# Taking the low part of a weight tile in two GpSimd operations of 512 columns instead of one of 1024

## The chip, the core and the metric

The kernel runs on one core of one Trainium2 chip. Time is device time in microseconds (us) of a whole launch, with all transfers. Five engines work side by side, each through its own list of instructions in a fixed order, and wait for each other by semaphores: TensorE (PE: matmuls, PEld: its weight loads), VectorE (DVE), ScalarE (ACT), GpSimd (POOL) and SyncE (SP, which only issues transfers here). An instruction whose inputs aren't ready holds up everything that stands behind it on its engine.

## What is computed

Three layers follow each other. The first is attention over 4 batches, 8 heads, 576 positions and 64 features per head, in which each query keeps only its 32 largest scores. The other two are MLPs over the 2304 tokens, 512 to 2048 to 512 features, each with its own gate. Cut to what matters:

```python
scores = scale * q @ k.T                       # per batch and head, 576 x 576
kth = partition(scores, -32)[..., -32]         # the 32nd largest of each row
attn = softmax(where(scores >= kth, scores, -1e9))
x = (attn @ v) as 2304 x 512
h = x @ w_in;  x = (h - tanh(h)) @ w_out                        # first MLP
h = x @ w_in;  x = where(h > 0, h, exp(min(h, 0)) - 1) @ w_out  # second MLP
```

## The kernel before

**Tokens in chunks.** The 2304 tokens go through in 6 chunks of 384. For each chunk, 4 pairs of heads are computed: scores `ps` (TensorE), copied to `s` (ScalarE), then four rounds of finding the 8 largest (`vm`, VectorE MAX8, line 406) and striking them out (`w`, VectorE, line 420), exponentials `e` (line 410 or 423 on ScalarE, masked on VectorE at line 427, or masked on ScalarE), transposes `pt` copied to `ph`, and the product `av` with the values. The result, normalised, is the chunk's `x`, kept as a high part `xh` and a low part `xl`. While one chunk's MLPs run on TensorE, the attention of later chunks runs on VectorE and ScalarE, so that the two share every engine.

**Numbers in two parts.** Matmuls take a number as high part plus low part. ScalarE copies the number into the rounded format (high), and GpSimd subtracts that from the number (low). The helper `split` does both, at lines 148 and 149, and so all of these operations have the same two lines in the profile: `gh` and `gl` (gated values), `kh`/`kl` in the tile `kk` (keys), `xl`, and the weights `wp`.

**The MLPs.** An MLP (`m` = 0 or 1) goes through 16 f-tiles (`ft`) of 128 hidden features. A step of it is: 12 matmuls of 384 columns at line 577 (`first`) into `h`, which has 2 buffers; a tanh or exponential `t` on ScalarE; a gate `g` on VectorE (line 596 in the first MLP, 591 in the second), which reads `h` and so releases its buffer; `gh` and `gl`; and 9 matmuls of 512 columns at line 613 (`second`) into `acc`. So `h` of step k+2 can't start before the gate of step k is done.

**The weights.** A f-tile's weights are a tile of 128 x 2 x 2 x 512: two halves of 512 columns (the first for `h`, the second for `acc`), each with a high and a low part. Chunk 0 makes them (`prepare`): a transfer brings the raw words `wr`; two operations on ScalarE (lines 186 and 203) and one on VectorE (line 189) make the number `wf` of 1024 columns out of them; ScalarE rounds it (`wp`, line 148), GpSimd takes the low part (`wp`, line 149), and a transfer at line 213 stores the whole tile. There are 32 of these, 16 for each MLP. All other chunks load the stored tiles (`wt`, line 222, 1 MB each) into a ring of 6 buffers. The first 12 tiles are made with the VectorE operation in two halves that read ScalarE's result from PSUM (`sc`); the 20 others with one of 1024 columns, both of whose inputs lie in SBUF.

**What sets the order.** The program is written in ticks, four for each group of query tiles, with tables that say in which tick each piece is written. Then a scheduler places the instructions on each engine by its own estimates of how long they take, so that an instruction which it thinks is longer or shorter moves its neighbours, and these theirs.

Of the kernel before, what the change touches and what calls it, by code (L numbers as in the profile page):

```python
# [106 lines left out]
def tile_topk_attention_two_mlps(  # L107
# [9 lines left out]
    nc = tc.nc  # L117
# [24 lines left out]
    copy = AF.Copy  # L142

    def f(ap):
        return ap.bitcast(F32)

    def split(hi, lo, src):
        nc.scalar.activation(hi, src, copy)  # L148
        return nc.gpsimd.tensor_sub(lo, src, f(hi))  # L149
# [7 lines left out]
    def bank(tag, name, bufs):  # L157
        if tag == "h":
            if "park" in pairs:
                turns.close()  # L160
                del pairs["park"]
                pairs["h"] = pool("ph", 1, PSUM)
            return pairs["h"].tile([P, 512], F32, tag=tag, name=name, bufs=bufs)
        return ps.tile([P, 512], F32, tag=tag, name=name, bufs=bufs)
# [7 lines left out]
    def weight_tile(name):  # L172
        return sb.tile([P, 2, 2, 512], F32R, tag="w", name=name, bufs=W2_BUFS)
# [3 lines left out]
    def prepare(m, ft):  # L177

        raw = sb.tile([P, 1024], I64, tag="wr", name=f"wr{m}_{ft}", bufs=RAW_BUFS)
        nc.sync.dma_start(raw, (w1, w2)[m][ft])  # L180
        words = raw.bitcast(F32).rearrange("p (n w) -> p n w", w=2)
        low, scaled = words.bitcast(U32)[:, :, 0], words[:, :, 1]
        w = sb.tile([P, 1024], F32, tag="wf", name=f"wf{m}_{ft}", bufs=WF_BUFS)

        def scale(out, src):
            nc.scalar.activation(out, src, AF.Prelu, scale=2.0**-112, alpha=-(2.0**32))  # L186

        def join(out, high, low):
            nc.vector.scalar_tensor_tensor(  # L189
                out.bitcast(U32), high.bitcast(U32), 3, low, op0=ALU.logical_shift_left, op1=ALU.bitwise_or  # L190
            )

        halves = [slice(0, 512), slice(512, 1024)]
        small = {}
        early = "wide" in stage
        if early:
            for a, cs in enumerate(halves):
                small[a] = bank(f"acc{stage['at'] % 3}", f"sc{m}_{ft}_{a}", 1)
                stage["at"] += 1
                scale(small[a], scaled[:, cs])  # L200
        else:
            scale(scaled, scaled)
        nc.scalar.activation(low.bitcast(I32), low, copy, scale=2.0**-29 * (1 - 2.0**-20), bias=-0.5 + 7.5 * 2.0**-20)
        if early:
            for a, cs in enumerate(halves):
                join(w[:, cs], small[a], low[:, cs])
        else:
            join(w, scaled, low)
        wt = weight_tile(f"wp{m}_{ft}")
        if m * NF + ft not in EARLY:  # L210
            weights[0, m, ft] = wt
        split(wt[:, :, 0], wt[:, :, 1], w.rearrange("p (h c) -> p h c", h=2))
        nc.sync.dma_start(f(scratch[m, ft]), f(wt))

    def load_next():
        if loads:
            ci, m, ft = loads.pop(0)
            if ci == 0 and m * NF + ft not in EARLY:
                prepare(m, ft)
                return  # L220
            wt = weights[ci, m, ft] = weight_tile(f"wt{ci}_{m}_{ft}")
            newest["weights"] = nc.sync.dma_start(f(wt), f(scratch[m, ft]))
# [508 lines left out]
    for tick in range(FIRST_TICK, n_ticks):  # L731
        for do in before.get(tick, ()):
            do()
        while early and PREP_AT + PREP_RATE * (len(EARLY) - len(early)) <= tick:
            i = early.pop(0)
            prepare(i // NF, i % NF)
# [16 lines left out]
        for j in range(max(1, len(todo))):  # L753
            a, b, c = todo[j] if todo else (lambda: None,) * 3
# [58 lines left out]
```

## Time and profile before

| | |
|---|---|
| runs | 1219.96, 1218.08, 1215.3 us |
| median of them | 1218.08 us |
| the profiled execution | 1219.57 us |
| its span, first to last instruction | 1217.8 us |
| TensorE busy | 1146.4 us, 94% of the span |
| VectorE busy | 944.5 us, 78% |
| ScalarE busy | 765.6 us, 63% |
| GpSimd busy | 497.9 us, 41% |
| mean granted TensorE clock | 0.973 |

The shares are means over unlike stretches. Up to about 150 us there is only attention and the making of weights, and TensorE is far from full. From 150 to about 215 us the first MLP of chunk 0 starts beside attention, VectorE is full, and TensorE has its last larger waits. From there on TensorE is busy 98% and more, and from about 1025 us there is little but MLPs.

### The profile page before, as it was taken

What the parts mean: (1) busy time and instruction counts of PE and PEld (TensorE: products, weight loads), DVE (VectorE), ACT (ScalarE), POOL (GpSimd) and SP (SyncE); (2) the same over time, 40 slices, a digit from 0 to 9 for tenths busy, and PEclk for the clock granted to TensorE, in tenths of its full rate; (3) what the DMA queues carried; (4) which work ended last, traced back from release to release, by engine and by line L of the source; (5) the groups of instructions that cost most, each with busy time, mean ns of one, the idle gap of its engine ahead of it and who ended that gap; (6) DMA issues with size and microseconds to landing.
All of it is one profiled execution on the core that took longest, in us unless ns stands there. A gap on an engine that the chain in (4) does not pass through costs nothing.

```text
span 1217.8 us, 18856 instructions
## 1 busy us (share of the span) xinstructions
PE 1146.4 (94%) x6349; PEld 977.0 (80%) x6349; DVE 944.5 (78%) x1898; ACT 765.6 (63%) x1594; POOL 497.9 (41%) x557
## 2 busy tenths in 40 slices
PE   6577689999999999999999999999999999999998
PEld 3344368888888979898978988988998888898887
DVE  7999999998999999679987789898889995100111
ACT  5999987888984555565664566575655564432333
POOL 2445446657753313443423444444334422333222
PEclk9688889999999999999999999999999999999999
DMA  7999937985979986669986779978688645686572
GB/s 246 398 333 330 311 111 276 350 266 217 356 285 327 276 294 184 238 166 299 241 182 234 242 204 260 251 219 266 225 241 243 204 127 207 210 283 248 198 269 95
DMA packets 81616, 301.69 MB, mean 248 GB/s; under 512 B 18800, under 2 KB 36080, under 8 KB 51696
## 3 DMA queue, kind: packets, MB, share of 16 engines
q1 hardware_dynamic: 81520, 300.49, 76.5%
q8 instruction: 50, 0.82, 0.3%
q14 instruction: 46, 0.38, 0.1%
HBM read 255.07 MB, written 45.39 MB: 247 GB/s over the span
## 4 chain that ended last, share of the span: by engine, by line
PE 75%; ACT 6%; DVE 5%; DMA 3%; issue 1%; POOL 1%; another core or an unknown queue 0%; ACTq 0%; DVEq 0%; POOLq 0%
PE h L577 30%; PE acc L613 30%; PE av L470 6%; PE pt L448 5%; DMA wt<-w 3%; PE ps L383 2%; PE ps L384 2%; DVE vm L406 2%; DVE w L420 2%; DVE wf L189 1%; ACT ph L449 1%; ACT s L385 1%; ACT e L410 1%; ACT y L627 1%; ACT wr L186 0%
## 5 line engine op out<-in xcount | busy, mean ns | idle before, releaser
L149 POOL TENSOR_TENSOR gl<-g,gh 128x384 fp32r<-128x384 f32 x192 | 205.3, 1071 | 385.0 <-ACT gh L148 360.2
L406 DVE MAX8 vm<-w 128x8 f32<-128x576 f32 x432 | 315.0, 748 | 3.1
L613 PE MATMUL acc<-wt,gh 128*128 128x512 f32 x1014 | 270.9, 398 | 0.3 <-ACT gh L148 0.3
L613 PEld LDWEIGHTS acc<-wt,gh 128*128 128x128 f32 x1014 | 186.2, 188 | 34.9 <-issue 3.3
L420 DVE MATCH_REPLACE8 w<-vm,w 128x576 f32<-128x576 f32 x288 | 212.7, 740 | 0.0
L148 ACT ACTIVATE gh<-g 128x384 fp32r<-128x384 f32 x192 | 100.7, 525 | 81.2 <-DVE g L591 34.6
L613 PE MATMUL acc<-wt,gl 128*128 128x512 f32 x507 | 148.9, 398 | 1.0 <-POOL gl L149 1.0
L577 PE MATMUL h<-zh,wt 128*128 128x384 f32 (+2 forms) x776 | 146.4, 324 | 2.4 <-ACT zh L632 2.0
L591 DVE SCALAR_TENSOR_TENSOR g<-t,h 128x384 f32<-128x384 f32 x96 | 52.2, 544 | 124.2 <-ACT t L583 123.8
L406 DVE MAX8 vm<-s 128x8 f32<-128x576 f32 x144 | 107.2, 750 | 47.1 <-ACT s L385 44.4
L577 PE MATMUL h<-xh,wt 128*128 128x384 f32 x672 | 140.9, 339 | 1.2 <-DMA wt<-w 1.2
L385 ACT ACTIVATE s<-ps 128x288 f32<-128x288 f32 (+1 forms) x272 | 107.5, 418 | 48.3 <-PE ps L384 40.7
L449 ACT ACTIVATE ph<-pt 116x384 f32<-116x384 f32 (+1 forms) x240 | 111.5, 499 | 40.0 <-PE pt L448 37.4
L448 PE MATMUL pt<-ident,e 128*116 128x128 f32 (+1 forms) x720 | 115.2, 288 | 22.7 <-ACT e L423 9.9
L577 PEld LDWEIGHTS h<-zh,wt 128*128 128x128 f32 x776 | 125.8, 189 | 8.8 <-ACT zh L632 3.2
L448 PEld LDWEIGHTS pt<-ident,e 128*116 128x116 f32 (+1 forms) x720 | 90.0, 142 | 43.2 <-ACT e L423 12.6
L577 PEld LDWEIGHTS h<-xh,wt 128*128 128x128 f32 x672 | 117.4, 188 | 7.5 <-ACT t L580 1.0
L582 ACT ACTIVATE t<-h 128x384 f32<-128x384 f32 x96 | 46.8, 489 | 119.7 <-PE h L577 119.7
L613 PEld LDWEIGHTS acc<-wt,gl 128*128 128x128 f32 x507 | 93.3, 188 | 19.9 <-POOL gl L149 1.2
L420 DVE MATCH_REPLACE8 w<-vm,s 128x576 f32<-128x576 f32 x144 | 106.7, 741 | 0.0
L596 DVE TENSOR_TENSOR g<-h,t 128x384 f32<-128x384 f32 x76 | 41.4, 545 | 70.6 <-ACT t L580 69.9
L580 ACT ACTIVATE t<-h 128x384 f32<-128x384 f32 x96 | 47.2, 492 | 75.1 <-PE h L577 74.6
(82 smaller groups left out, 1938.7 us busy)
## 6 DMA issues: line engine op xcount, KB each, us to landing
wt<-w SPq DMA_DIRECT2D x169, 1024.0 KB, 6.5
wr<-in_w_dram SPq DMA_DIRECT2D x32, 1024.0 KB, 7.2
w<-wp SPq DMA_DIRECT2D x32, 1024.0 KB, 8.5
kraw<-in_kT_dram SPq DMA_DIRECT2D x96, 144.0 KB, 6.2
vraw<-in_vL_dram SPq DMA_DIRECT2D x64, 160.0 KB, 4.5
sd<-sp SPq DMA_DIRECT2D x24, 288.0 KB, 7.3
s<-sd SPq DMA_DIRECT2D x24, 288.0 KB, 9.0
qraw<-in_qT_dram SPq DMA_DIRECT2D x64, 96.0 KB, 5.7
```

Source lines behind the costliest of these rows:

```text
L148: nc.scalar.activation(hi, src, copy)
L149: return nc.gpsimd.tensor_sub(lo, src, f(hi))
L385: nc.scalar.activation(s[lo:hi, cs], pt[lo:hi, :HS], copy)
L406: nc.vector.max(g.vm[:, j, min(r, 1)], u.s[t] if r == 0 else g.w[j])
L420: nc.vector.match_replace(g.w[j], v, u.s[t] if r == 0 else g.w[j], FILL)
L448: nc.tensor.transpose(pt[:kn, j * P : j * P + P], v.e[t][:, k0 : k0 + kn], ident)
L449: nc.scalar.activation(g.ph[:kn, blk, :nq], pt[:kn, :nq], copy)
L470: nc.tensor.matmul(banks[c0][h * D : h * D + D, : v.n], v.vraw[h][:kn, blk], v.g.ph[:kn, blk, cs], start=(blk == order[0]), stop=(blk == o ...
L577: nc.tensor.matmul(h[:, cs], wv[:, wi, kt], xs[:, kt, cs], start=(a == 0), stop=(a == len(jobs) - 1))
L580: nc.scalar.activation(t, h, AF.Tanh)
L591: nc.vector.scalar_tensor_tensor(g, t, -1.0, h, op0=ALU.add, op1=ALU.max)
L613: nc.tensor.matmul(acc[ci, m][t], gx[:, t * P : t * P + P], wt[:, wi], start=(ft == 0 and k == 0), stop=(ft == NF - 1 and k == 2),)
```

## The change

In `prepare` the call of `split` is written out. The operation on ScalarE is the same as before, one of 1024 columns. The subtraction on GpSimd becomes two, one for each half of 512 columns; both wait for the one operation on ScalarE, and the transfer that stores the tile waits for both. `halves` and `copy` were there before, and `f` reads a tile as plain 32-bit numbers.

```diff
-        split(wt[:, :, 0], wt[:, :, 1], w.rearrange("p (h c) -> p h c", h=2))
+        nc.scalar.activation(wt[:, :, 0], w.rearrange("p (h c) -> p h c", h=2), copy)
+        for a, cs in enumerate(halves):
+            nc.gpsimd.tensor_sub(wt[:, a, 1], w[:, cs], f(wt[:, a, 0]))
         nc.sync.dma_start(f(scratch[m, ft]), f(wt))
```

Line numbers of later code move by two (406 becomes 408, and so on). The scheduler also places other instructions differently: TensorE's list is the same up to the place that was executed at 172.5 us, differs in 2041 of its 5895 places from there to the one executed at 615.1 us, and is the same again after that. The lists of VectorE, ScalarE and GpSimd differ over about the same stretch (VectorE's has one exchange of neighbours at 59.6 us besides).

GpSimd's list where chunk 0's first MLP starts, before (names end in the f-tile and a running number: `wp_6` is the weights of f-tile 6):

```order
L149 TENSOR_TENSOR gl_0_2_1703<-g_0_2_1700,gh_0_2_1702 128x384
L149 TENSOR_TENSOR wp_6_1656<-wf_6_1652,wp_6_1656 128x2x512
L149 TENSOR_TENSOR gl_0_3_1774<-g_0_3_1771,gh_0_3_1773 128x384
L149 TENSOR_TENSOR wp_7_1739<-wf_7_1735,wp_7_1739 128x2x512
L326 TENSOR_TENSOR qs_2_0_384_0_2089<-qraw_2_0_384_0_1874,qs_2_0_384_0_2089 64x384
L149 TENSOR_TENSOR kk_2_0_384_0_0_2092<-kraw_2_0_384_0_0_1877,kk_2_0_384_0_0_2092 128x576
L149 TENSOR_TENSOR wp_8_1804<-wf_8_1800,wp_8_1804 128x2x512
```

And now:

```order
L214 TENSOR_TENSOR wp_6_1671<-wf_6_1667,wp_6_1671 128x512 x2
L149 TENSOR_TENSOR gl_0_2_1719<-g_0_2_1716,gh_0_2_1718 128x384
L214 TENSOR_TENSOR wp_7_1755<-wf_7_1751,wp_7_1755 128x512 x2
L328 TENSOR_TENSOR qs_2_0_384_0_2110<-qraw_2_0_384_0_1893,qs_2_0_384_0_2110 64x384
L149 TENSOR_TENSOR kk_2_0_384_0_0_2113<-kraw_2_0_384_0_0_1896,kk_2_0_384_0_0_2113 128x576
L149 TENSOR_TENSOR gl_0_3_1791<-g_0_3_1788,gh_0_3_1790 128x384
```

The two halves stand directly behind each other, and each `wp` stands one `gl` earlier.

VectorE's list some 15 us earlier, where the last pair of heads of chunk 0 is finished (`xun` is its product, which waits for the matmuls `av`), before:

```order
L420 MATCH_REPLACE w_0_1_0_0_384_0_2_1446<-vm_0_1_0_0_384_0_1441,s_0_0_384_0_2_1313 128x576
L406 MAX vm_0_1_0_0_384_0_1441<-w_0_1_0_0_384_0_1_1445 128x8
L406 MAX vm_0_1_0_0_384_0_1441<-w_0_1_0_0_384_0_2_1446 128x8
L482 TENSOR_TENSOR xun_3_1426<-av_3_0_1427,rs_3_1424 128x384
L420 MATCH_REPLACE w_0_1_0_0_384_0_2_1446<-vm_0_1_0_0_384_0_1441,w_0_1_0_0_384_0_2_1446 128x576
```

And now:

```order
L422 MATCH_REPLACE w_0_1_0_0_384_0_2_1458<-vm_0_1_0_0_384_0_1453,s_0_0_384_0_2_1323 128x576
L484 TENSOR_TENSOR xun_3_1438<-av_3_0_1439,rs_3_1436 128x384
L408 MAX vm_0_1_0_0_384_0_1453<-w_0_1_0_0_384_0_1_1457 128x8
L408 MAX vm_0_1_0_0_384_0_1453<-w_0_1_0_0_384_0_2_1458 128x8
L408 MAX vm_0_1_0_1_0_0_1610<-s_0_1_0_0_0_1464 128x8
```

`xun` now stands ahead of two MAX that stood ahead of it.

VectorE's list between the gates of f-tiles 4 and 5, before:

```order
L596 TENSOR_TENSOR g_0_4_1846<-h_0_4_1823,t_0_4_1836 128x384
L420 MATCH_REPLACE w_1_1_1_0_384_0_1_1887<-vm_1_1_1_0_384_0_1883,s_1_0_384_0_1_1683 128x576
L406 MAX vm_1_1_1_0_384_0_1883<-w_1_1_1_0_384_0_0_1886 128x8
L427 SCALAR_TENSOR_TENSOR e_0_1_0_0_2_1662,sum_0_1_0_1_0_0_1597<-s_0_1_0_0_2_1514,vm_0_1_0_1_0_0_1595,e_0_1_0_0_2_1662 128x576
L420 MATCH_REPLACE w_1_1_1_0_384_0_2_1888<-vm_1_1_1_0_384_0_1883,s_1_0_384_0_2_1762 128x576
L406 MAX vm_1_1_1_0_384_0_1883<-w_1_1_1_0_384_0_1_1887 128x8
L189 SCALAR_TENSOR_TENSOR wf_10_1937<-wr_10_1935 128x1024
L596 TENSOR_TENSOR g_0_5_1918<-h_0_5_1889,t_0_5_1902 128x384
```

And now, without the gate of f-tile 4 ahead of it:

```order
L422 MATCH_REPLACE w_1_1_1_0_384_0_1_1906<-vm_1_1_1_0_384_0_1902,s_1_0_384_0_1_1699 128x576
L408 MAX vm_1_1_1_0_384_0_1902<-w_1_1_1_0_384_0_0_1905 128x8
L429 SCALAR_TENSOR_TENSOR e_0_1_0_0_2_1678,sum_0_1_0_1_0_0_1612<-s_0_1_0_0_2_1528,vm_0_1_0_1_0_0_1610,e_0_1_0_0_2_1678 128x576
L422 MATCH_REPLACE w_1_1_1_0_384_0_2_1907<-vm_1_1_1_0_384_0_1902,s_1_0_384_0_2_1779 128x576
L408 MAX vm_1_1_1_0_384_0_1902<-w_1_1_1_0_384_0_1_1906 128x8
L422 MATCH_REPLACE w_1_1_1_0_384_0_0_1905<-vm_1_1_1_0_384_0_1902,w_1_1_1_0_384_0_0_1905 128x576
L408 MAX vm_1_1_1_1_0_0_2218<-s_1_1_1_0_0_0_1928 128x8
L408 MAX vm_1_1_1_0_384_0_1902<-w_1_1_1_0_384_0_2_1907 128x8
L422 MATCH_REPLACE w_1_1_1_0_384_0_1_1906<-vm_1_1_1_0_384_0_1902,w_1_1_1_0_384_0_1_1906 128x576
L189 SCALAR_TENSOR_TENSOR wf_10_1956<-wr_10_1954 128x1024
L408 MAX vm_1_1_1_0_384_0_1902<-w_1_1_1_0_384_0_0_1905 128x8
L598 TENSOR_TENSOR g_0_5_1937<-h_0_5_1908,t_0_5_1921 128x384
```

The gate of f-tile 5 stands five instructions further back, three MAX and two MATCH_REPLACE.

## Rows read from the trace of the kernel before

**Rows 1.** Busy time by stretch: us, then each engine's busy us, clock, DMA.

```profile
core 0: us, PE busy (x) PEld busy (x) DVE busy (x) ACT busy (x) POOL busy (x), PEclk, DMA share, GB/s
150.00:205.00 55.00, 47.87 (x243) 40.29 (x244) 53.04 (x100) 42.97 (x87) 30.93 (x31) 0.89 0.51 168
205.00:360.00 155.00, 152.17 (x980) 133.34 (x980) 148.04 (x284) 136.74 (x268) 98.85 (x99) 1.00 0.83 294
360.00:650.00 290.00, 287.16 (x1615) 246.37 (x1614) 260.76 (x548) 162.52 (x351) 103.84 (x134) 1.00 0.83 249
```

**Rows 2.** GpSimd's groups: mean, idle before; then a line's min/median/max in ns.

```profile
L149 POOL TENSOR_TENSOR kk<-kraw,kk 128x576 fp32r<-128x576 f32 x48 | 68.6, 1430 | 36.2 <-ACT kk L148 32.2 <-PE pt L448 2.7
...
L149 POOL TENSOR_TENSOR wp<-wf,wp x32: 2355/2390/3398, 23.1 to 355.1; 128x1024 fp32r<-128x1024 f32 x32
```

**Rows 3.** VectorE's operations with two SBUF inputs: min/median/max in ns.

```profile
L189 DVE SCALAR_TENSOR_TENSOR wf<-wr x20: 1195/1216/3120, 110.5 to 349.2; 128x1024 uint32<-128x1024 uint32 x20
...
L427 DVE SCALAR_TENSOR_TENSOR e<-s,vm,e x99: 790/808/1623, 149.4 to 1022.8; 128x576 f32<-128x576 f32 x99
```

**Rows 4.** Timeline of GpSimd and VectorE, 188 to 200 us: start, us, instruction.

```profile
188.40 2.39 POOL L149 TENSOR_TENSOR wp<-wf,wp 128x1024 fp32r<-128x1024 f32 x1
...
194.23 2.39 POOL L149 TENSOR_TENSOR wp<-wf,wp 128x1024 fp32r<-128x1024 f32 x1
...
188.83 3.03 DVE L189 SCALAR_TENSOR_TENSOR wf<-wr 128x1024 uint32<-128x1024 uint32 x1
...
194.58 3.12 DVE L189 SCALAR_TENSOR_TENSOR wf<-wr 128x1024 uint32<-128x1024 uint32 x1
```

**Rows 5.** Timeline of GpSimd and VectorE near 351 us.

```profile
350.01 2.62 POOL L149 TENSOR_TENSOR wp<-wf,wp 128x1024 fp32r<-128x1024 f32 x1 [5.21 <-ACT wp L148]
352.58 1.53 POOL L149 TENSOR_TENSOR gl<-g,gh 128x384 fp32r<-128x384 f32 x1
...
351.62 1.62 DVE L427 SCALAR_TENSOR_TENSOR e<-s,vm,e 128x576 f32<-128x576 f32 x1
```

**Rows 6.** Timeline of ScalarE and TensorE, 197 to 203 us, and the clock there.

```profile
197.79 1.06 ACT L148 ACTIVATE wp<-wf 128x1024 fp32r<-128x1024 f32 x1 [4.33 <-DVE wf L189]
...
199.28 0.48 PE L383 MATMUL ps<-kk,qs 128*128 128x288 f32 x1 [2.24 <-ACT ph L449]
...
199.20:202.90 3.70, 3.35 (x10) 3.01 (x11) 3.70 (x9) 3.70 (x6) 2.28 (x2) 0.54 1.04 343
```

**Rows 7.** Timeline of VectorE around `xun`.

```profile
165.50 1.41 DVE L406 MAX8 vm<-w 128x8 f32<-128x576 f32 x2
168.53 0.56 DVE L482 TENSOR_TENSOR xun<-av,rs 128x384 f32<-128x384 f32 x1 [1.62 <-PE av L470]
```

**Rows 8.** Timeline of VectorE and TensorE, 204 to 210 us.

```profile
204.79 0.54 DVE L596 TENSOR_TENSOR g<-h,t 128x384 f32<-128x384 f32 x1
...
208.70 0.53 DVE L596 TENSOR_TENSOR g<-h,t 128x384 f32<-128x384 f32 x1
...
206.51 1.55 PE L577 MATMUL h<-xh,wp 128*128 128x384 f32 x8
...
208.59 0.85 PE L613 MATMUL acc<-wp,gl 128*128 128x512 f32 x3
209.29 0.82 PE L448 MATMUL pt<-ident,e 128*116 128x128 f32 x6
209.86 1.63 PE L577 MATMUL h<-xh,wp 128*128 128x384 f32 x8
```

**Rows 9.** The longest wait of TensorE for GpSimd.

```profile
304.89 0.97 PE L613 MATMUL acc<-wt,gl 128*128 128x512 f32 x3 [0.99 <-POOL gl L149]
```

**Rows 10.** Timeline of VectorE and TensorE, 525 to 530 us.

```profile
525.29 0.76 DVE L406 MAX8 vm<-s 128x8 f32<-128x576 f32 x1 [3.60 <-ACT s L385]
525.97 0.53 DVE L591 SCALAR_TENSOR_TENSOR g<-t,h 128x384 f32<-128x384 f32 x1
...
529.47 0.59 PE L577 MATMUL h<-xh,wt 128*128 128x384 f32 x2
```

## Prediction

> **What bounds the kernel now.** I read the busy time by stretch first, since the change sits in the first third only. From 150 to 205 us VectorE is busy 53.0 of 55 us and TensorE 47.9: VectorE is the bound there, and TensorE waits for it. From 205 to 360 us TensorE is busy 152.2 of 155, from 360 to 650 us 287.2 of 290 [rows 1]. So up to about 215 us a microsecond of VectorE counts, and later one counts only where TensorE comes to wait. After 615 us the lists of instructions are the same as before, and before 172 us nearly so; what the change can do, it does between.
>
> The second view is the duration of single operations, min to max. VectorE's line 189 takes 1.20 us at least and 3.12 at most, line 427 0.79 and 1.62 [rows 3]. These two read two operands from SBUF. Both long ones of line 189 lie in the same place: they began 0.43 and 0.35 us after a GpSimd operation on `wp` of 2.39 us, and ended 1.08 us after that one had ended, at 190.79 and 196.62 [rows 4]. That is a wait of 1.8 and 1.9 us inside the operation, for GpSimd's to finish. The reader is to see in the next rows that it goes on: ScalarE stood 4.33 us before the next `wp`, waiting for that `wf`, with the copy of `ph` behind it, and TensorE waited 2.24 us for `ph`, and came back at a granted clock of 0.54, near the lower of its two levels (1.2 of 2.4 GHz) [rows 6]. This is the largest wait of TensorE that a `wp` of 1024 columns has a hand in.
>
> **The change part by part.**
>
> *GpSimd's own time.* No row has 512 columns. 576 columns take 1.43 us, 1024 take 2.39 [rows 2], so a column costs 0.96/448 = 2.14 ns and 512 columns 1.43 - 64 x 0.00214 = 1.29 us. Two are 2.58, 0.19 more than one of 1024, and 32 times that is 6.1 us. The bounds are 0.47 more per tile (two of 576) and nothing (if the halves run into each other without a seam). GpSimd is busy 98.9 of 155 us in its fullest stretch [rows 1], and TensorE's longest wait for it is 0.99 us [rows 9]. On the path I count 0; if each tile that is wanted at once cost its 0.19, a few of them would give under 1 us.
>
> *What VectorE waits inside its operations.* If GpSimd gives way between the halves, the two waits of [rows 4] end with the first half: 2.39 - 1.29 = 1.10 us earlier each, 2.2 us together. That it gives way where its next instruction is already in line is shown once: `gl` at 352.58 took 1.53 us behind a `wp`, while line 427 ended 0.62 us after that `wp` [rows 5]. So I take 2.2. One end of the range is 3.7 (1.8 + 1.9: in the new order the operations don't meet at all), the other +0.4 (VectorE waits for both halves, 2 x 0.19 longer). A line 427 that meets a second half, as the one at 351.62 would, gains nothing.
>
> On this a page of the Trainium skill bears: "SBUF — State Buffer", section "SBUF: two separate sides", has it that VectorE with two SBUF inputs and GpSimd hold a shared port for a whole instruction and that the other is blocked; [rows 4] agree. "GPSIMD Engine Reference", section "Instruction dispatch", speaks against the change: a GpSimd core starts the next Pool instruction as soon as its share of the last is done, so that two halves in a row need not leave a gap. By the first page's rule the sum has -2.2, by the second's it would have +0.4; [rows 5] are why I go with the first page.
>
> *What the new order does from 166 to 216 us.* Here VectorE is the bound, so I follow it to the gate of f-tile 5. (a) `xun` now stands ahead of two MAX of 1.41 us together, and it waits for `av`, which ends at 168.5 whatever stands ahead [rows 7]: VectorE idles 1.4 us more. (b) The two waits, -2.2. (c) Five more instructions stand ahead of this gate, three MAX and two MATCH_REPLACE, about 0.7 us each from start to start: +3.5. The gate ended at 204.79 + 0.54 = 205.33 [rows 8], and will at 205.33 + 1.4 - 2.2 + 3.5 = 208.0. TensorE's `h` of f-tile 7 takes the buffer that this gate releases. It began at 206.51 and will at 208.0. Behind it the loss is made good in part: three matmuls of `acc` (0.70 us from start to start) and six transposes (0.57), which stood between the `h` of f-tiles 7 and 8 [rows 8], now stand ahead of both, in time in which TensorE waits anyway. So `h` of f-tile 8 is reached at 208.0 + 2.1 (its 12 matmuls, 206.51 to 208.59) + 0.3 (three transposes that have come between) = 210.4. Its own buffer comes free with the gate of f-tile 6, which stands three places further back than before (five minus two): 208.70 + 0.53 + 1.4 - 2.2 + 2.1 = 210.5. Against 209.86 this is 0.6 us later, with 0.3 us of transposes done: **+0.4 us** on the path. The 2.24 us of TensorE's wait in [rows 6] are not a gain of their own, since VectorE sets the end of this stretch; what is next late behind them is the gate. The bounds: without any meeting -1.1, with a wait for both halves +3.0.
>
> *From 216 to 360 us.* The second MLP of chunk 0 has its gates up to ten instructions earlier in VectorE's list, and `gl` of f-tile 4 in GpSimd's ahead of two `wp` that it stood behind. TensorE's 0.99 us at 304 [rows 9] should go: **-1.0 us**, between 0 and -1.4.
>
> *From 360 to 615 us.* Nothing of the making of weights is left here; instructions only change places, on TensorE by up to 4 us of its work. I count 0, and up to 3 us either way: TensorE's whole idle time there is 2.8 us [rows 1].
>
> The sum is 0 + 0.4 - 1.0 = -0.6 us on the span, 1217.2, and with the 1.77 us that lie around it 1219.0 for this execution. It stands 1.5 us above the median of the runs, so against that median I forecast **1217.5 us**. The bounds of the terms give 1213 to 1222. A measurement of this kernel can tell about 0.5%, 6 us, from no change, so this is "the same".
>
> **The rivals.**
>
> *Faster: VectorE and GpSimd no longer meet, and VectorE stops being late.* `wp` of f-tiles 7 and 8 stand elsewhere in GpSimd's list than the operations they met. Then (b) is 3.7, the stretch to 216 us gives -1.1 instead of +0.4; without an idle time ahead of it, TensorE doesn't come back at half its clock, which cost 3.7 us at 0.54 [rows 6], some 1.3 us after what idled; the two line-427 operations that met a `wp` (0.8 us each, 1.6 in all) go; and of the 2.8 us idle from 205 to 360 us [rows 1] all goes. -1.1 - 1.3 - 1.6 - 2.8 = -6.8: 1211.3. For it: each term has its row. Against it: the gates stand further back, and `wf` of f-tile 9 is still made about when `wp` of f-tile 8 is split.
>
> *Slower: gates that come too late for TensorE after 490 us.* The gate at 525.97 ended 2.97 us before TensorE began the `h` that takes its buffer, at 529.47 [rows 10]. In the new order 11 more VectorE instructions stand ahead of it, 7.9 us, and TensorE has 1.5 us more to do until that `h`: 3.4 us short. The following four gates are moved by 8 to 13 places, so it isn't made good at once. At f-tile 8 of the same MLP I count 2.2 us in the same way. VectorE idled 3.60 us just ahead of the MAX at 525.29 [rows 10], which covers the 3.4 if the instructions moved up have their inputs by then, and nothing if they wait for the same late scores. It decides whether the scores come earlier too. Uncovered: 3.4 + 2.2 + 0.4, without the -1.0: +6 us, 1224.1, and up to 1226.7 with both halves waited for.
>
> *No gap between the halves.* GpSimd keeps the operands until the second half is done. Then (b) is +0.4 and the stretch costs 3.0: 1220.1, still "the same". [rows 5] speak against it, though there the two GpSimd instructions aren't of one tile.
>
> That the change doesn't do what it says is out: in the new list every `wp` stands as two of 128 x 512.
>
> **How the numbers follow.** The forecast within its bounds has 0.48, no gap 0.09, both "the same". Faster by over 0.5% (under 1212.0) has 0.23, slower (over 1224.2) 0.20. The range leaves out about 0.1 on either side, the outer halves of the two: 1209.5 to 1226.
>
> **What would show it.** The operations on 512 columns at 1.29 us, 64 of them, GpSimd's busy time up by 6 us. No line 189 over some 2.3 us. `h` of f-tile 7 beginning near 208 us after a wait for a gate, f-tile 8 near 210.5, and from there TensorE as full as before. The 0.99 us near 304 gone. The gates near 526 us shown as the last wait of TensorE, if the slower case is right. I am wrong if line 189 still takes 3 us and more, if TensorE is more than 3 us earlier or later by 216 us, or if it idles by more than 3 us anywhere from 360 to 615.

## The result

The changed kernel took 1224.96 us (median of 5 runs, 1223.35 to 1226.57), the kernel before 1217.0 beside it; the ratio is 1.0066 (95% interval 1.0044 to 1.0087), so it is slower by 8 us. Its profiled execution took 1225.37 us, with a span of 1223.6, 5.8 us more than the span of the kernel before.

The busy time by stretch of the changed kernel (us, then each engine's busy us, clock, DMA) answers to [rows 1]:

```profile
150.00:205.00 55.00, 46.11 (x247) 39.39 (x248) 54.97 (x108) 44.65 (x93) 31.32 (x33) 0.92 0.51 156
205.00:360.00 155.00, 148.14 (x936) 129.07 (x934) 145.86 (x271) 134.53 (x261) 103.03 (x111) 0.98 0.86 308
360.00:650.00 290.00, 287.81 (x1626) 246.45 (x1627) 261.29 (x544) 161.56 (x353) 100.87 (x133) 1.00 0.81 238
```

TensorE's idle time in 205 to 360 us rose from 2.8 to 6.9 us, and behind 360 it is as full as before. So the loss lies in one stretch. Matching the two traces matmul by matmul (the k-th of one with the k-th of the other) says the same more sharply: the changed kernel stands 1.4 us behind at 293 us, 5.6 at 310, 5.6 at 619, where the lists become equal, and 5.8 at the end. A lag of about 2 us isn't the change's by itself: at 150 us, ahead of the place where TensorE's lists part, this trace is 1.8 us behind, and those of the later runs with either list lie between 0.3 ahead and 2.6 behind. The step of 4.3 us from 293 to 310 us is larger than that.

The durations of GpSimd's and VectorE's operations (min/median/max in ns) answer to [rows 2] and [rows 3]:

```profile
L214 POOL TENSOR_TENSOR wp<-wf,wp x64: 1262/1284/2275, 22.6 to 355.1; 128x512 fp32r<-128x512 f32 x64
...
L189 DVE SCALAR_TENSOR_TENSOR wf<-wr x20: 1204/1226/2302, 110.5 to 348.8; 128x1024 uint32<-128x1024 uint32 x20
...
L429 DVE SCALAR_TENSOR_TENSOR e<-s,vm,e x99: 793/810/1820, 151.2 to 1028.6; 128x576 f32<-128x576 f32 x99
```

A half takes 1.28 us, and the longest line 189 is 2.30 us where it was 3.12. What the change was cut for has come about; it isn't where the time went. Two lines further down in the file, the same places of the code have numbers that are 2 higher (line 429 is 427 of before).

The timeline of the changed kernel from 295 to 310 us (start, us, engine, instruction, in brackets the idle time before it and what ended it) has the largest wait of TensorE behind 205 us:

```profile
295.52 2.06 POOL L328 TENSOR_TENSOR qs<-qraw,qs 64x384 fp32r<-64x384 f32 x1
...
298.04 1.44 POOL L149 TENSOR_TENSOR kk<-kraw,kk 128x576 fp32r<-128x576 f32 x1
...
299.45 1.02 POOL L149 TENSOR_TENSOR gl<-g,gh 128x384 fp32r<-128x384 f32 x1
...
300.63 6.00 POOL L214 TENSOR_TENSOR wp<-wf,wp 128x512 fp32r<-128x512 f32 x4
...
303.20 0.33 SPq L215 DMA_DIRECT2D w<-wp  x1
303.20 2.30 DVE L189 SCALAR_TENSOR_TENSOR wf<-wr 128x1024 uint32<-128x1024 uint32 x1 [1.67 <-ACT t L584]
...
305.43 1.82 DVE L429 SCALAR_TENSOR_TENSOR e<-s,vm,e 128x576 f32<-128x576 f32 x1
...
305.60 1.06 ACT L212 ACTIVATE wp<-wf 128x1024 fp32r<-128x1024 f32 x1 [1.83 <-DVE wf L189]
...
306.56 0.51 ACT L585 ACTIVATE t<-t 128x384 f32<-128x384 f32 x1
...
308.70 0.55 DVE L593 SCALAR_TENSOR_TENSOR g<-t,h 128x384 f32<-128x384 f32 x1
...
309.31 2.93 PE L579 MATMUL h<-zh,wp 128*128 128x384 f32 x8 [4.58 <-DVE g L593]
```

In the kernel before, the gate of the same f-tile and the matmuls that take the buffer it releases are these, with no wait ahead of the matmuls:

```profile
306.57 0.54 DVE L591 SCALAR_TENSOR_TENSOR g<-t,h 128x384 f32<-128x384 f32 x1
...
307.47 1.55 PE L577 MATMUL h<-zh,wp 128*128 128x384 f32 x8
```

Read the first of the two from below. TensorE waits 4.58 us for the gate of f-tile 5 of chunk 0's second MLP, which ends 2.1 us later than in the kernel before. The gate stands on VectorE behind line 189 for f-tile 10, an `e` on line 429, a MAX and a MATCH_REPLACE. Line 189 writes the buffer that the low part of f-tile 8's weights still reads; the four halves in a row are those of f-tiles 8 and 9, f-tile 8's second one ends at about 303.2, where the transfer that stores that tile is issued (SPq), and there line 189 begins. (The view names ScalarE's `t` as what ended the 1.67 us, which ended at the same moment; the traces of two later runs name `wp`.) Inside, line 189 meets a half of f-tile 9, and `e` the last half. On ScalarE the second part of the activation of f-tile 5, which the gate needs, stands behind a `wp` that waits for that line 189. And the halves of f-tile 8 came late since GpSimd's list now has `qs` and `kk` of a unit of the next chunks, and `gl`, ahead of them.

TensorE's own list may have a part in the wait as well. The matmuls that wait stand 13 places earlier in it than in the kernel before: nine transposes and four matmuls of scores that stood ahead of them now stand behind. From the first matmul of f-tile 6's `h` to the first of f-tile 7's TensorE is busy 3.8 us, where it was busy 6.9. No run below moves an instruction of TensorE alone, so whether it makes the wait longer, and by how much, isn't shown.

TensorE pays for the wait twice: it comes back at half its clock, and the eight matmuls take 2.93 us where they took 1.55. The window of the 2.8 us behind it (PE, PEld, DVE, ACT, POOL busy, then the granted clock):

```profile
309.30:312.10 2.80, 2.79 (x9) 2.80 (x10) 2.73 (x5) 2.78 (x6) 1.08 (x2) 0.50 0.98 360
```

### The profile page after: what moved, and what is told of

Same layout as the page of the kernel before. It is cut to its first block, busy times and chain, and to the rows that moved or that the text cites. A ratio compares the mean times of both kernels' runs of the same rounds, so it can differ in the third digit from the quotient of the medians.

```text
span 1223.6 us, 18887 instructions
## 1 busy us (share of the span) xinstructions
PE 1146.4 (94%) x6349; PEld 976.0 (80%) x6349; DVE 948.6 (78%) x1898; ACT 764.0 (62%) x1594; POOL 501.8 (41%) x589
## 4 chain that ended last, share of the span: by engine, by line
PE 75%; ACT 9%; DMA 6%; DVE 6%; issue 2%; POOL 1%; SPq 0%; another core or an unknown queue 0%; ACTq 0%; POOLq 0%; DVEq 0%
PE h L579 30%; PE acc L615 30%; PE av L472 5%; PE pt L450 4%; DMA wr<-in_w_dram 4%; DVE vm L408 3%; DVE w L422 2%; PE ps L385 2%; PE ps L386 2%; ACT ph L451 1%; ACT s L387 1%; DMA wt<-w 1%; ACT wr L203 1%; ACT sc L186 1%; DVE wf L189 1%
## 5 line engine op out<-in xcount | busy, mean ns | idle before, releaser
L149 POOL TENSOR_TENSOR gl<-g,gh 128x384 fp32r<-128x384 f32 x192 | 202.2, 1055 | 384.7 <-ACT gh L148 370.3
L408 DVE MAX8 vm<-w 128x8 f32<-128x576 f32 x432 | 319.4, 751 | 3.4
```

Of the source, the lines that this page charges most:

```text
L408: nc.vector.max(g.vm[:, j, min(r, 1)], u.s[t] if r == 0 else g.w[j])
```

## The experiments

**Which part: the halves or the order.** The order in which an engine issues can be fixed: after all instructions are recorded, each is tied to the one ahead of it on its engine by an edge that asks for issue order alone, no wait. The orders come from the two built programs, written down as lists of places.

```diff
+    for a, b in zip(at, at[1:]):
+        tc.add_manual_dep(
+            todo[b], todo[a].name, mybir.DependencyInfo(mybir.DependencyClass.NoSync, mybir.DependencyReason.DATA), reason="order"
+        )
```

With this the kernel of halves runs in the order of before on all engines, and the kernel of one operation in the order of the changed one. Two more join the lists at about 271 us, where on each engine the same set of instructions stands ahead in both.

Halves in the old order. 

> Two GpSimd operations of 512 columns for each weight tile, as in the changed kernel, but every engine issues its instructions in the order of the kernel before (the two halves stand side by side where the one operation stood). Theory 'order' (the 7 us are the price of the new order alone): the time of before within 2 us, 1215 to 1219, ratio 0.998 to 1.002. Theory 'halves' (GpSimd is held longer, since a VectorE operation that comes in between the halves stretches the second to 2.3 us: 3.5 us for a tile instead of 2.4): 1221 to 1225, ratio 1.003 to 1.007. In both, line 189 should be 2.3 us at most where it was 3.1, and the waits of VectorE in operations that meet a wp should fall by some 2 us in sum.

One operation in the new order. 

> One GpSimd operation of 1024 columns, as in the kernel before, but every engine issues its instructions in the order of the changed kernel. Theory 'order': the time of the changed kernel, 1223 to 1227, ratio to before 1.005 to 1.008, with a wait of TensorE for a gate of about 4 to 5 us near 308 us. Theory 'halves': 1215 to 1219, and no wait of TensorE over 1.5 us there. If both are needed, it lies between, and so does the run with the halves in the old order.

Halves; old order up to 271 us, new order behind it. 

> Halves; the order of before up to about 271 us, that of the changed kernel from there to the end. In the two traces TensorE of the changed kernel was about 2 us behind at 271 us, 1.4 behind at 293, 5.6 behind after 309 and stayed there. If the order from 271 us on holds the loss by itself (theory 'late gate': the gate of f-tile 5 of chunk 0's second MLP is late whatever comes before): 3.5 to 5.7 us over before, 1220.5 to 1222.7, with the wait of about 4.6 us for that gate. If the lateness is brought along from the stretch before 271 us (theory 'inherited'): within 2 us of before, and no wait over 2 us for that gate.

Halves; new order up to 271 us, old order behind it. 

> Halves; the order of the changed kernel up to about 271 us, that of the kernel before from there on: the counterpart of the run with the old order first. TensorE of the changed kernel was 2.3 us behind at 269 us, of which the opening, before the orders part, had 1 to 2. If the loss sits in the list behind 271 us, as that run has it (ratio 1.0056): within 2.5 us of before, 1215.5 to 1219.5, ratio 0.999 to 1.0025, and no wait for the gate near 305 us over 1 us. If the first stretch costs as much again: 1220 and more.

Measured, with TensorE's busy time of the 155 us from 205 to 360 us and its wait for the gate near 305 us:

| kernel | ratio to before | 95% interval | TensorE busy, us | wait for the gate, us |
|---|---|---|---|---|
| halves, old order | 1.0008 | 0.9998 to 1.0019 | 151.98 | none over 0.2 |
| one operation, new order | 1.0050 | 1.0037 to 1.0063 | 148.27 | 4.03 |
| halves, old then new | 1.0056 | 1.0042 to 1.0070 | 149.56 | 3.87 |
| halves, new then old | 1.0015 | 1.0004 to 1.0026 | 150.79 | 0.20 |
| changed kernel (halves, new order) | 1.0066 | 1.0044 to 1.0087 | 148.14 | 4.58 |

The order makes the loss, the halves as such next to nothing (0.2% at most), and most of it lies in the list behind 271 us. Two times are a little off what was expected with this: the run of one operation took 1222.05 us, under 1223 to 1227, and that with the old order first 1223.51, over 1220.5 to 1222.7. In the timeline of the run with one operation the same wait stands, and line 189 ahead of it now meets a whole `wp`:

```profile
300.96 3.40 DVE L189 SCALAR_TENSOR_TENSOR wf<-wr 128x1024 uint32<-128x1024 uint32 x1 [1.55 <-ACT e L422]
...
307.15 2.93 PE L577 MATMUL h<-zh,wp 128*128 128x384 f32 x8 [4.03 <-DVE g L591]
```

and in that of the run with the old order first, the trace names GpSimd's `wp` for the idle time ahead of line 189:

```profile
301.20 2.31 DVE L189 SCALAR_TENSOR_TENSOR wf<-wr 128x1024 uint32<-128x1024 uint32 x1 [1.69 <-POOL wp L214]
...
307.31 2.93 PE L579 MATMUL h<-zh,wp 128*128 128x384 f32 x8 [3.87 <-DVE g L593]
```

**Is it the place of the gate?** The changed kernel with these instructions moved:

```
ScalarE:  t of f-tile 5 (585) right behind its line 584;
          t of f-tile 6 (584, 585) and gh of f-tile 5 ahead of wp of f-tile 10
VectorE:  g of f-tile 5 ahead of line 189 for f-tile 10, g of f-tile 6 right behind it
GpSimd:   gl of f-tile 5 ahead of the halves of f-tile 10
```

> The changed kernel with six instructions moved: on ScalarE the second part of the activation of f-tile 5 (line 585) right behind its first, and both parts for f-tile 6 and gh of f-tile 5 ahead of the wp of f-tile 10; on VectorE the gate of f-tile 5 ahead of line 189 for f-tile 10 and that of f-tile 6 right behind it; on GpSimd gl of f-tile 5 ahead of that wp's halves. Theory 'late gate' (these stood behind a wf that waited 1.67 us for its buffer and 1.1 for GpSimd, and behind top-k work): the wait of 4.58 us at 309 goes to under 1 us, and the time falls by 2 to 5 us against the changed kernel, to 1220 to 1223. Rival: TensorE then waits as long for the next gate or for the weights of f-tile 10 (all is late there, not this chain): within 1 us of the changed kernel, 1224 to 1226.

The rival held: ratio 1.0079 (1.0066 to 1.0091), no faster than the changed kernel. TensorE takes the gate without a wait and stands 4.39 us before the next matmuls of scores, as its timeline shows:

```profile
308.57 0.78 ACT L425 ACTIVATE e<-e,b 128x576 f32<-128x576 f32 x1 [0.75 <-POOL b L416]
...
312.58 0.61 PE L385 MATMUL ps<-kk,qs 128*128 128x288 f32 x1 [4.39 <-ACT s L387]
```

The copies of scores that it needs stand on ScalarE behind an `e` that waits for `b`, and `b` stands on GpSimd behind the same four halves. That wait is 0.75 us of ScalarE's time; two operations on the weights of a later f-tile (186 and 203) and a second `e` stand between as well. So these copies were moved too:

```
ScalarE:  three copies of scores (387) ahead of that e (425)
```

> The run with the gates of f-tiles 5 and 6 moved forward, where TensorE waited 4.39 us for ScalarE's copy of scores instead; here three of these copies (line 387) stand on ScalarE ahead of the e that waits for GpSimd's b. Theory 'a queue of late work' (each thing that TensorE needs there stands behind operations that wait for the halves of f-tiles 8 and 9): this wait goes as well, and no wait of TensorE from 300 to 320 us is over 1.5 us; 1219 to 1222, ratio 1.003 to 1.005. Rival: the next in line is as late, and the time stays at 1224 to 1226.

Half of each in the waits, and the rival's in the time: the waits at 309 and 312 are gone, and near 310 us TensorE is only 1.1 us behind the kernel before; by 316 us it is 4.4 behind again, and two new waits show:

```profile
314.00 0.54 PE L450 MATMUL pt<-ident,e 128*116 128x128 f32 x3 [1.10 <-ACT s L387]
...
317.75 1.67 PE L615 MATMUL acc<-wp,gh 128*128 128x512 f32 x6 [1.61 <-ACT gh L148]
```

The time is 1.0055 (1.0043 to 1.0067), 1224.36 us. Moving what TensorE waits for moves the wait.

**Is VectorE's own work late, or GpSimd's?** Here 15 instructions of VectorE work on half the columns, and nothing moves (cut to what matters):

```diff
+LIGHT = "1_3_1_3_0_384_0"
-            nc.vector.max(g.vm[:, j, min(r, 1)], u.s[t] if r == 0 else g.w[j])
+            few = slice(0, 288) if r and g.id == LIGHT else slice(0, S)
+            nc.vector.max(g.vm[:, j, min(r, 1)], u.s[t] if r == 0 else g.w[j][:, few])
```

(and the MATCH_REPLACE alike). 

> The changed kernel in its own order, where 15 of VectorE's MAX and MATCH_REPLACE of one unit (1_3, first part of its heads, about 281 to 301 us) work on 288 of 576 columns; the selection of that unit leaves out the other columns. That takes some 5 us of VectorE's work out of the stretch just ahead of the late gate, and moves nothing. Theory 'VectorE's list' (its own work makes the gate late): the wait of 4.58 us falls by 3 us and more, and the time by 3 to 5 us against the changed kernel, to 1219 to 1222. Theory 'GpSimd's list' (line 189 for f-tile 10 waits for the buffer that GpSimd gives back): VectorE stands longer ahead of that line 189 (4 us and more instead of 1.67), the wait for the gate stays over 3.5 us, 1223 to 1225.

GpSimd's list rather than VectorE's: 1.0062 (1.0044 to 1.0079), the wait for the gate as long as it was, and VectorE standing 3.20 us for `wp` where it stood 1.67 (4 us and more were expected). From 278 us to this line VectorE's work is 3.9 us less (21.2 to 17.3) and its idle time 4.0 us more, so that what was saved is spent waiting:

```profile
302.44 2.30 DVE L190 SCALAR_TENSOR_TENSOR wf<-wr 128x1024 uint32<-128x1024 uint32 x1 [3.20 <-POOL wp L215]
...
308.55 2.93 PE L582 MATMUL h<-zh,wp 128*128 128x384 f32 x8 [4.53 <-DVE g L596]
```

**GpSimd's list alone.** `qs` and `kk` of unit 3 moved behind the halves of f-tile 9:

```
GpSimd was:  wp7 wp7 qs nk b kk gl mb wp8 wp8 wp9 wp9 b wp10 wp10
       is:   wp7 wp7 nk b gl mb wp8 wp8 wp9 wp9 qs kk b wp10 wp10
```

> The changed kernel with two GpSimd instructions moved and nothing else: qs and kk of unit 3 stand behind the halves of f-tiles 8 and 9 of the second MLP's weights instead of ahead of them (they took 3.5 us, and the next operation of TensorE that needs them is far off). Theory 'GpSimd's list' (VectorE's line 189 for f-tile 10 stands 1.67 us for the buffer that f-tile 8's second half gives back, then 1.1 inside for a half of f-tile 9, and the next operation 1.0; ScalarE and the gate stand behind it): the wait for the gate of 4.58 us falls to 1 to 3 us, the time by 1.5 to 4 us against the changed kernel, ratio to before 1.003 to 1.0055. Rival (VectorE's and ScalarE's own lists are what makes it late): as the changed kernel within 1 us, wait over 4 us.

The wait for the gate fell as forecast, to 2.32 us, and the time rose to 1.0113 (1.0094 to 1.0131). The profiled execution is the fastest of the five, 1227.32 us. Its timeline has two reasons, both of the place that I chose for the two:

```profile
303.58 1.11 SPq L303 DMA_DIRECT2D qraw<-in_qT_dram  x2
...
304.75 1.66 PE L579 MATMUL h<-zh,wp 128*128 128x384 f32 x8 [2.32 <-DVE g L593]
304.80 0.52 SPq L180 DMA_DIRECT2D wr<-in_w_dram  x1
...
305.23 0.78 ACT L425 ACTIVATE e<-e,b 128x576 f32<-128x576 f32 x1 [2.50 <-POOL b L416]
...
311.00 1.10 ACT L186 ACTIVATE wr<-wr 128x1024 f32<-128x1024 f32 x1 [4.52 <-DMA wr<-in_w_dram]
...
314.19 0.61 PE L385 MATMUL ps<-kk,qs 128*128 128x288 f32 x1 [7.08 <-ACT s L387]
```

`b` stands behind the two and comes 2.5 us late. And `qs` gives back the buffer that the next load of q takes: on SP the load of f-tile 11's weights stands behind that load and went out at 304.80 instead of 298.83, and ScalarE waited 4.52 us for it. So both were put right in the next run: `qs` and `kk` behind the halves of f-tile 10, and on SP the loads of q and k behind those of the weights.

```
GpSimd:  wp7 wp7 nk b gl mb wp8 wp8 wp9 wp9 b wp10 wp10 qs kk
SP was:  q q wr11 k k w8 wr12 w9 w10        (w8: the store of f-tile 8's parts)
   is:   wr11 w8 wr12 w9 w10 q q k k
```

> The changed kernel with qs and kk of unit 3 moved on GpSimd behind the halves of f-tiles 8, 9 and 10 (in the run that moved them behind f-tile 9 the wait for the gate fell from 4.58 to 2.32 us, as forecast, but b stood behind them, and the load of f-tile 11's weights stood on SP behind loads of q and k that wait for the two; ScalarE waited 4.5 us for that load, TensorE 7.1). Here the loads of q and k stand on SP behind the load of f-tile 12 as well, and b ahead of the two. Theory 'GpSimd's list': both waits shrink, the gate's to 1 to 3 us, the other to under 1.5; 1219 to 1223, ratio 1.0025 to 1.005. Rival 'VectorE's list': VectorE is as late at the end of this stretch, TensorE waits somewhere up to 330 us, and the time stays at 1224 to 1226.

Held in the waits: the one for the gate is 1.70 us, and no other is over 0.6 from 295 to 345 us. In the profiled execution TensorE loses 1.7 us from 293 to 310 us, where the changed kernel loses 4.3. The time is 1.0047 (1.0028 to 1.0066), as forecast, but its interval overlaps that of the changed kernel (1.0044 to 1.0087): that the kernel as a whole is faster by it isn't shown.

```profile
306.02 1.65 PE L579 MATMUL h<-zh,wp 128*128 128x384 f32 x8 [1.70 <-DVE g L593]
```

All moves together. 

> The same moves on GpSimd and SP, with those of the gates of f-tiles 5 and 6 and of the copies of scores on ScalarE and VectorE. Theory 'GpSimd's list': no wait of TensorE over 1.5 us from 300 to 330, TensorE 1 to 2.5 us behind the kernel before at 330 us instead of 5.5; 1217.5 to 1221, ratio 1.001 to 1.0035. Rival 'VectorE's list': 1223 to 1226 as each of these moves alone gave it.

A miss: 1.0049 (1.0031 to 1.0066), no better than GpSimd's and SP's moves alone. TensorE was level with the kernel before at 310 us (0.35 us behind) and 3.6 behind at 316, by the waits for copies and `gh` that the run with the gates and copies had. In this trace ScalarE is busy 14.7 of the 15 us from 303 to 318 us, and `gh` stands in its list behind `t` (585), two operations on weights (186 and 203) and copies of `ph`. So here what TensorE waits for stands in line on ScalarE behind work, and not behind a wait for GpSimd; in the kernel before ScalarE is as full (14.9 of 15 us from 300 to 315). No run tried another order on it.

**More pieces.** Four operations of 256 columns, once as the scheduler orders them, once in the order of before:

```diff
-        for a, cs in enumerate(halves):
-            nc.gpsimd.tensor_sub(wt[:, a, 1], w[:, cs], f(wt[:, a, 0]))
+        for j in range(4):
+            a, cs = j // 2, slice(256 * (j % 2), 256 * (j % 2) + 256)
+            nc.gpsimd.tensor_sub(wt[:, a, 1, cs], w[:, 256 * j : 256 * j + 256], f(wt[:, a, 0, cs]))
```

> Four GpSimd operations of 256 columns for each tile, in the order that the scheduler makes of them, which is neither that of before nor that of the changed kernel (about 2,000 places of TensorE's list differ from either); here qs and kk of unit 3 do not stand ahead of the halves of f-tile 8. Theory 'order': what counts is where the list puts things, and not the number of pieces; without that pile-up 1214 to 1221. Theory 'pieces' (each further cut costs): slower than the changed kernel, 1226 to 1232.

> Four operations of 256 columns in the order of the kernel before, on every engine. By the halves' cost (1.29 us for 512 columns against 2.39 for 1024, so 0.2 us for each further piece) a tile takes 2.9 to 3.1 us, 20 us of GpSimd's time more in all. Theory 'order': 1215 to 1219, ratio 0.998 to 1.003, as the halves in this order. Theory 'pieces': 1222 and more.

Both went against the theory of the order as I had put it, the second by little. In the scheduler's order: 1.0065 (1.0053 to 1.0078), although nothing piles up near 300 us; this list loses 4.3 us elsewhere, from 443 to 490 us, where TensorE is busy 41.87 of 47 us instead of 46.18 and waits for another `e` and another gate:

```profile
465.12 0.54 PE L451 MATMUL pt<-ident,e 128*116 128x128 f32 x3 [2.21 <-DVE e L430]
...
485.21 1.65 PE L580 MATMUL h<-zh,wt 128*128 128x384 f32 x8 [1.16 <-DVE g L594]
```

So it is a third order with a loss of its own, and no proof that any order but the old one is free. In the old order: 1.0031 (1.0019 to 1.0042), between the two theories. The pieces do have a price once they are small: 0.734 us each, 2.94 for a tile against 2.39, and the wait for `gl` of [rows 9], 0.99 us in the kernel before, is 2.75 here. With halves in the old order the same wait is 1.22.

```profile
L215 POOL TENSOR_TENSOR wp<-wf,wp x128: 720/734/1806, 22.9 to 362.3; 128x256 fp32r<-128x256 f32 x128
```

```profile
309.09 1.65 PE L616 MATMUL acc<-wt,gl 128*128 128x512 f32 x3 [2.75 <-POOL gl L149]
```

## Why the prediction was wrong

The time lies in the range of 1209.5 to 1226.0, but the forecast was no change, and slower by over 0.5% had only 0.20. That the range holds it is luck: it reached that far for a rival whose loss lay elsewhere. Step by step:

- *GpSimd's own time: right for a half.* 1.29 us was worked out, 1.28 measured. All `wp` took 8.3 us more (78.0 to 86.3), where 6.1 was the estimate, since a half that meets VectorE is longer; GpSimd's busy time as a whole rose by 3.9 us (497.9 to 501.8). That this lies on no path to within 0.2% is shown by the run with halves in the old order, 1.0008 (0.9998 to 1.0019).
- *What VectorE waits inside its operations: right in its mechanism, and half of it overlooked.* VectorE does get in between the halves. In the changed kernel's timeline

```profile
190.02 3.53 POOL L214 TENSOR_TENSOR wp<-wf,wp 128x512 fp32r<-128x512 f32 x2
...
190.28 2.12 DVE L189 SCALAR_TENSOR_TENSOR wf<-wr 128x1024 uint32<-128x1024 uint32 x1
```

  the first half, at its 1.28 us, ended at 191.30, line 189 at 192.40, and the second half only at 193.55. So line 189 waited for one half, 0.9 us instead of 1.8, and the rival "no gap" is out. Here the two pages that the prediction weighed part. "SBUF — State Buffer", section "SBUF: two separate sides", of the Trainium skill has the port held for a whole instruction, and these rows agree: held for one, given over behind it. What the prediction took from "GPSIMD Engine Reference" of the Trainium skill, section "Instruction dispatch", for a reason against the change (the next instruction starts at once) costs nothing here. Overlooked was the other side: the second half takes 2.25 us instead of 1.28, so a tile that is met keeps GpSimd for 3.53 us, not 2.58, and whoever stands behind it on GpSimd is a microsecond later.
- *The new order from 166 to 216 us: the number right, the path not.* `h` of f-tile 7 was forecast to begin at 208.0 and of f-tile 8 at 210.5, and in the timeline they do:

```profile
166.82 0.55 DVE L484 TENSOR_TENSOR xun<-av,rs 128x384 f32<-128x384 f32 x1
...
203.14 2.83 PE L615 MATMUL acc<-wp,gh 128*128 128x512 f32 x6 [1.92 <-ACT gh L148]
...
206.46 0.53 DVE L598 TENSOR_TENSOR g<-h,t 128x384 f32<-128x384 f32 x1
...
208.11 1.63 PE L579 MATMUL h<-xh,wp 128*128 128x384 f32 x8
...
210.52 1.64 PE L579 MATMUL h<-xh,wp 128*128 128x384 f32 x8
```

  But VectorE doesn't idle ahead of `xun` (1.4 us more were forecast), and the gate of f-tile 5 ends at 206.99 and not at 208.0. Neither `h` waits for a gate: TensorE is late by 1.92 us of waiting for ScalarE's `gh` at 203.14, behind which six matmuls take 2.83 us instead of 1.67. That the sum of this step comes out is luck.

- *From 216 to 360 us: this step failed.* It gave -1.0 us; the traces show +4 to +5 (1.2 us behind at 216 us and 5.6 at 310 in the changed kernel, 0.0 and 4.9 in the run of one operation in its order). I had counted by how many places the gates move up in VectorE's list and `gl` in GpSimd's, and took that for earlier. What it left out: that the halves of f-tile 8 now stand on GpSimd behind `qs`, `kk` and `gl`; that line 189 for f-tile 10 needs the buffer that they give back; and that the gate stands behind this line 189, whatever its number in the list (the gate of f-tile 5 stands two places further up than before, this line 189 four, and the gate ends 2.1 us later). It left out TensorE's own list too, which comes to the matmuls that wait with 13 fewer ahead of them. The 0.99 us of [rows 9] did go, but there is a wait of the same kind earlier:

```profile
216.25 0.96 PE L615 MATMUL acc<-wp,gl 128*128 128x512 f32 x3 [1.15 <-POOL gl L149]
```

  For the direction I relied on TensorE's idle time of 2.8 us in the stretch [rows 1]. That bounds what can be gained there. It bounds no loss, with VectorE busy 148 of 155 us and GpSimd, as the runs show, without room around 300 us.
- *From 360 to 615 us: right.* 0 was forecast; TensorE is 5.6 us behind at 310 us and 5.6 at 619. In between the lag swings between 4.5 and 8.2 us, as the two lists put the same work in different places.
- *The rivals.* The slower one had nearly the time, 1224.1, and its mechanism, gates too late for TensorE; but it had put it behind 490 us, in the gates near 526, where TensorE waits for no gate. The right kind of loss at the wrong place is why it got only 0.20: I had looked for gates that move back, and the one that came late had moved up.

Open is what is left: with `qs` and `kk` out of the way on GpSimd and SP the new order still costs 0.28 to 0.66%, of which the list up to 271 us holds 0.04 to 0.26%. Some 1.7 us are the wait that remains for the gate; what TensorE's own list has to do with it, and what the rest is, no run tried. No run beats the kernel before; halves in its order are level with it.

## What to carry to other kernels

A change that costs nothing by itself can still reshuffle a scheduled kernel, and then the order is the change: fix the order, run old work in the new order and new work in the old, and it is known in two runs which of them has the time. When an order is read, follow for each late gate what its list has ahead of it down to the buffer that it waits for, on every engine and on the queue that issues the loads; a higher place in one list says nothing if the instruction ahead waits for another list. If moving the instruction that is waited for only moves the wait, look for the list that all the waits have in common.

## What the runs showed of the hardware that was not expected

When VectorE meets GpSimd between two pieces, it isn't free: VectorE gains 0.9 us and the second piece takes 1.0 us longer. In all, the time that lines 189 (of 1024 columns) and 429 spend over the median of their kind hardly changed: 17.2 us before, 17.6 in the changed kernel and 16.6 with halves in the old order, where a fall of some 2 us had been expected.

On VectorE, an instruction that reads what its neighbour has just written starts later. Over the whole changed kernel 95 of the 253 MATCH_REPLACE right behind a MAX start 0.11 to 0.12 us after that one's end, and the other 158 start 0.01 to 0.03 before it. Of the 263 MAX right behind a MATCH_REPLACE, 101 start 0.03 to 0.04 after its end and 157 start 0.07 to 0.09 before it. A MATCH_REPLACE at 201.95 us, behind the MAX of another tile, is one of those that start before (0.02). In the timeline of the changed kernel the chain of one tile, in which each reads what the one ahead has written, has the late starts and runs at 0.8 us from start to start, where the two MAX of different tiles ahead are 0.68 apart:

```profile
293.96 0.76 DVE L408 MAX8 vm<-w 128x8 f32<-128x576 f32 x1
294.64 0.74 DVE L408 MAX8 vm<-s 128x8 f32<-128x576 f32 x1
...
298.34 0.74 DVE L422 MATCH_REPLACE8 w<-vm,w 128x576 f32<-128x576 f32 x1
299.12 0.76 DVE L408 MAX8 vm<-w 128x8 f32<-128x576 f32 x1
...
300.00 0.74 DVE L422 MATCH_REPLACE8 w<-vm,w 128x576 f32<-128x576 f32 x1
300.77 0.76 DVE L408 MAX8 vm<-w 128x8 f32<-128x576 f32 x1
```

In the part of VectorE's list that the kernel before runs from 169 to 307 us the new order has 29 such late starts where the old one has 20. At 0.11 to 0.13 us each that is an estimate of 1.1 us of VectorE's time; no run tried it apart.
